# Three pairs of blocks taken through a two-level Strassen–Winograd feed-forward in lockstep, with every weight product streamed from DRAM

## The chip, the cores and the metric

The kernel runs on one core of a Trainium2 chip. The metric is the device time of that core in microseconds, as the median of three runs. Each version also has one profiled execution, whose span (first to last instruction) and own time stand beside the median below. In the profile PE is TensorE's matmuls, PEld its weight loads (which overlap the matmuls), DVE is VectorE, ACT ScalarE, POOL GpSimd and SP SyncE. All arithmetic is fp32. Names such as `x`, `h`, `t` and `r` are tiles in SBUF; `m`, `a`, `b` and `c` are PSUM pools.

## The reference

A linear attention without a softmax, then a gated feed-forward network, on 8 sequences of 576 positions with 8 heads of 64. The two are joined by laying the heads side by side.

```python
kv  = np.einsum('bhsd,bhse->bhde', k, v)          # one 64x64 matrix per sequence and head
out = np.einsum('bhsd,bhde->bhse', q, kv)
rms = np.sqrt(np.mean(out * out, axis=-1, keepdims=True) + 1e-06)
x   = (out / rms * g_norm).transpose(0, 2, 1, 3).reshape(4608, 512)
g   = x @ w_gate                                   # [4608,512] @ [512,1536]
val = x @ w_val
res = (g * (1.0 / (1.0 + np.exp(-g))) * val) @ w_out   # [4608,1536] @ [1536,512]
```

## The kernel before

**Blocks.** The 4608 tokens are worked in nine blocks of 512 (`NB = 9`, `BLK = 512`), numbered 0 to 8. For each block there is an `Att` object, which makes the block's `x` [512 features × 512 tokens, features on the partitions], and an `Ffn` object, which has an *up* part (gate and value products, silu, their product `h`) and a *down* part (`h @ w_out`). Blocks run one after the other; while block n's feed-forward runs, pieces of block n+1's attention are put between its products.

**Strassen–Winograd.** A product of 2 × 2 blocks of matrices can be made with seven smaller products instead of eight, at the price of sums of the operands and of the results. The kernel's up does this at no level for block 0 (`plain_up`, line 1026: matmuls with 512 columns of tokens, in two runs of 256), at one level for block 1 (class `Up`, line 587: 256 columns), and at two levels from block `DEEP = 2` on (class `Inner`, line 660). At two levels there are 49 products of 128 × 128 × 128, each named by an outer number and an inner number from 1 to 7. For one pair `d` of the six 128-wide weight columns, `Inner` runs four groups of outer products, `GROUPS = ((1, 5), (6, 2), (7,), (4, 3))`, and in each group the inner products 1, 5, 6, 2 and 7 with 3 and 4 of the group before put in between (`sequence`, line 701). The product with outer `o` and inner `p` has a leaf of the weights as its stationary operand (`weight`, line 704) and a leaf of x as its moving operand of 128 columns (`operand`, line 712). It is done for the two columns f = 0, 1 of the pair. So one step of a group with two outers makes four products, which fill one PSUM bank of 512 columns. Inner products accumulate in three chains of PSUM tiles, `a`, `b` and `c`. A finished bank is moved out by ScalarE for group 0 and by an add on VectorE for the others (`multiply`, line 719: the `L111` and `L742` rows of the profile), and the last combinations (`made1` to `made3`) run on GpSimd and ScalarE. The final one writes `h` and its sums `s1`.

**Down.** One level, seven products of 12 matmuls with 256 columns (line 565, of class `Quad`; class `Down`, line 855). Three of them (5, 7, 4) need differences of `w_out`, which `turn_t` makes on GpSimd, for each block anew, in tiles of the pool `t`. During down the next block's attention is finished: `fill[p]()` in `Ffn.down` (line 998) runs the steps that `Att.steps` names. After product 1 come the heads (line 361), the squares, the root of the norm, its scaling and a transpose on VectorE; after product 5, `place_x` issues 16 DMAs that put the 32 × 32 pieces of the transposed x in place, eight of them on SP and eight on ScalarE's queue; after product 2, `end` applies the gain and makes the sums of x that both Strassen levels need (`sums`, line 443), which end in the tiles `x` and `xi`.

**Weights.** The original leaves and the sums of the four outer numbers 1, 6, 2, 3 with inner 1, 6, 2, 3 are resident in `wg` and `wv`. The other 33 leaves of each column live in DRAM, written by block 1 (`leaf_steps`, line 829), and are streamed for every block. Class `Stream` (line 787) holds a queue of chunks of mostly 256 KB, 17 per pair of columns, in the order of use (`CHUNKS`). The pool `t` has nine tiles of this size. `pump` (line 801) issues one DMA on SP for each tile that has come free; it is called after every product. `enable` opens a block's chunks after product 7 of the down before.

**What sets the order.** Every engine takes its instructions in the order of the program, as the scheduler lays it out from the code and the explicit `issue_after` constraints. TensorE thus takes products, k/v visits (`visit`: `kv`, line 305, whose matmuls are at line 316) and heads in a fixed order. SP takes all loads in one order: weight chunks (line 809), k and v (`load_kv`, line 257), q and the stores of results (line 953). q comes by `load_quarters` (line 271, the DMA at line 284): 32 DMAs for a block, in pieces of 32 positions × 32 of a head's 64 elements. `load_q` issues all 16 of one half; in block 2's up block 4's q is issued in four lots of about eight. Afterwards block n+2's q is issued together ahead of block n's down. In block 1's up, block 3's q is issued after the second k/v visit.

**Room.** `x` and `xi` come from the pool `x`, `h` from the pool `h`, each with one buffer, so the next block's x is written when the last product of this block's up has been read, in down.

## Time and profile before

| | |
|---|---|
| runs | 1020.94, 1022.35, 1024.27 us; median 1022.35 us |
| profiled execution | 1020.91 us, its span 1019.1 us |
| granted TensorE clock | 0.999 |
| matmul instructions | 8522 |
| VectorE, GpSimd, ScalarE instructions | 1169, 280, 353 |
| moved by DMA | 170.26 MB, 167 GB/s in the mean |
| weight chunks (`t<-w`) of 256 KB | 336, 3.5 us from issue to landing |

Of the stretches of the trace, block 2's up runs from 269.5 us to 338.9 us and its down to 377.1; the next blocks begin their up at 377.1, 484.4, 591.8, 699.0, 808.8 and 913.3 us, so that a block takes 107.3 us in blocks 3, 4 and 5, 109.7 in block 6 and 104.5 in block 7. The last down ends at 1015.7 us.

How to read it: the busy table counts an instruction from start to end, and since matmuls are pipelined with modelled ends, the distance between the starts of two of them is the better price of one. A row of the timeline has the start in microseconds, the length of the run of like instructions, engine, line, operation, tile written and read, sizes and count; a time in brackets with an arrow is idle time before it and what released it. SPq are the DMAs that SP issues, and their length there is the time that SP needs to issue them, not the time until the data have landed. In the group rows, "L728 PE" is the two-level up, "L565 PE" the one-level up and all downs. Line 111 is the helper for sums, line 112 that for differences and line 113 that for products, so their rows gather many places; the tile names tell them apart.

### The profile page before, as it was taken

The page shows a single profiled execution, that of the slowest core. Times are in us where ns is not written, and L with a number is a line of the kernel's source. Part 1 is how long each engine was busy: PE and PEld are TensorE (multiplying, and loading weights), DVE is VectorE, ACT ScalarE, POOL GpSimd, SP SyncE. Part 2 cuts the span into 40 slices and gives each one's busy share as a digit, 9 for nine tenths or more (in the row PEclk, how much of TensorE's full clock was granted, in tenths as well). Part 3 has the DMA queues.
Part 4 walks back from the last instruction along what each step waited for, and adds up shares of the span by engine and source line. Part 5 has one row for each costly group of instructions (what it writes and reads, how often), then busy time and mean ns, then how long its engine had stood idle before and what let it go on. Part 6 is the DMA issues. An engine that isn't in the chain of part 4 may idle for free.

```text
span 1019.1 us, 21397 instructions
## 1 busy us (share of the span) xinstructions
PE 1003.5 (98%) x8522; PEld 895.9 (88%) x8522; DVE 700.9 (69%) x1169; ACT 228.1 (22%) x353; POOL 368.9 (36%) x280
## 2 busy tenths in 40 slices
PE   6999999999999999999999999999999999999998
PEld 4544688888999899998999899988998999989997
DVE  3999688998666946685558566665668466946661
ACT  2765112121211221221121111111121211221110
POOL 0000263534055503561246315630555045513670
PEclk9999999999999999999999999999999999999999
DMA  8689643767888277846685568646772766066601
GB/s 238 202 257 273 119 81 109 188 165 159 251 231 244 50 195 202 248 83 147 206 234 136 101 207 241 168 62 194 233 201 44 182 191 192 22 169 199 194 25 42
DMA packets 273844, 170.26 MB, mean 167 GB/s; under 512 B 150608, under 2 KB 241872, under 8 KB 273744
## 3 DMA queue, kind: packets, MB, share of 16 engines
q1 hardware_dynamic: 238800, 164.42, 59.1%
q10 hardware_dynamic: 34880, 4.46, 2.7%
q8 instruction: 68, 1.11, 0.5%
q14 instruction: 32, 0.26, 0.1%
q0 software_dynamic: 64, 0.00, 0.0%
HBM read 138.02 MB, written 22.41 MB: 157 GB/s over the span
## 4 chain that ended last, share of the span: by engine, by line
PE 90%; DVE 6%; DMA 2%; issue 1%; ACT 1%; SPq 0%; DVEq 0%; ACTq 0%
PE b L728 26%; PE b L565 19%; PE c L728 13%; PE c L565 10%; PE a L728 6%; PE a L565 5%; PE b L1035 4%; PE c L1035 4%; PE m L361 1%; PE m L316 1%; DVE r L112 1%; DVE r L111 1%; DVE xi L112 1%; DMA h<-in_v_dram 1%; DVE t L112 1%
## 5 line engine op out<-in xcount | busy, mean ns | idle before, releaser
L111 POOL TENSOR_TENSOR r<-r 128x256 f32<-128x256 f32 (+1 forms) x105 | 110.7, 1061 | 295.2 <-DVE r L111 292.9
L111 DVE TENSOR_TENSOR r<-b,r 128x512 f32<-128x512 f32 (+1 forms) x273 | 161.9, 605 | 64.9 <-PE b L728 60.4
L112 POOL TENSOR_TENSOR t<-wo 128x512 f32<-128x512 f32 x81 | 114.4, 1436 | 211.9 <-DVE wo L111 102.6
L111 DVE TENSOR_TENSOR r<-c,r 128x512 f32<-128x512 f32 (+1 forms) x179 | 108.3, 616 | 89.1 <-PE c L728 58.2
L728 PE MATMUL b<-x,t 128*128 128x128 f32 x1092 | 151.2, 275 | 0.0
L111 DVE TENSOR_TENSOR r<-a,r 128x512 f32<-128x512 f32 (+1 forms) x99 | 62.4, 630 | 113.1 <-PE a L565 71.2
L728 PEld LDWEIGHTS b<-x,t 128*128 128x128 f32 x1092 | 136.5, 192 | 0.8 <-DVE r L111 0.2
L728 PE MATMUL c<-xi,t 128*128 128x128 f32 x840 | 112.4, 275 | 1.0 <-DVE xi L111 1.0
L113 POOL TENSOR_TENSOR h<-r 128x1024 f32<-128x1024 f32 (+1 forms) x40 | 82.4, 2075 | 82.2 <-DVE r L111 79.2
L728 PEld LDWEIGHTS c<-xi,t 128*128 128x128 f32 x840 | 102.9, 192 | 1.2 <-DVE xi L111 1.2
L565 PE MATMUL b<-wo,h 128*128 128x256 f32 x432 | 100.1, 383 | 0.1
L565 PE MATMUL b<-t,h 128*128 128x256 f32 x432 | 96.2, 379 | 0.0
L565 PEld LDWEIGHTS b<-t,h 128*128 128x128 f32 x432 | 82.0, 190 | 11.3 <-issue 0.2
L565 PEld LDWEIGHTS b<-wo,h 128*128 128x128 f32 x432 | 79.8, 190 | 13.2 <-DVE h L113 2.5
L742 ACT COPY r<-b 128x512 f32<-128x512 f32 x63 | 36.9, 585 | 214.9 <-PE b L728 208.1
L728 PE MATMUL b<-xi,t 128*128 128x128 f32 x588 | 79.7, 276 | 0.0
L728 PEld LDWEIGHTS b<-xi,t 128*128 128x128 f32 x588 | 72.4, 192 | 0.0
L728 PE MATMUL b<-x,wg 128*128 128x128 f32 x336 | 52.8, 279 | 0.2 <-DVE x L112 0.2
L728 PE MATMUL b<-x,wv 128*128 128x128 f32 x336 | 51.2, 275 | 0.0
L565 PE MATMUL a<-wo,h 128*128 128x256 f32 x216 | 48.3, 379 | 0.0
L565 PE MATMUL c<-t,s 128*128 128x256 f32 x216 | 48.1, 379 | 0.0
L565 PE MATMUL c<-wo,h 128*128 128x256 f32 x216 | 48.1, 379 | 0.0
(133 smaller groups left out, 1562.2 us busy)
## 6 DMA issues: line engine op xcount, KB each, us to landing
t<-w SPq DMA_DIRECT2D x336, 256.0 KB, 3.5
out_dram<-r SPq DMA_DIRECT2D x17, 512.0 KB, 3.1
ld<-in_k_dram SPq DMA_DIRECT2D x26, 288.0 KB, 4.9
ld<-in_v_dram SPq DMA_DIRECT2D x26, 288.0 KB, 5.8
ld<-in_moe_w_gate_dram SPq DMA_DIRECT2D x12, 512.0 KB, 4.7
ld<-in_moe_w_val_dram SPq DMA_DIRECT2D x12, 512.0 KB, 4.6
ld<-in_moe_w_out_dram SPq DMA_DIRECT2D x12, 512.0 KB, 5.0
w<-t SPq DMA_DIRECT2D x18, 256.0 KB, 3.0
```

The source lines that it names most:

```text
L111: add = lambda e, o, a, b: e.tensor_tensor(out=o, in0=a, in1=b, op=OP.add)
L112: sub = lambda e, o, a, b: e.tensor_tensor(out=o, in0=a, in1=b, op=OP.subtract)
L113: mul = lambda e, o, a, b: e.tensor_tensor(out=o, in0=a, in1=b, op=OP.mult)
L316: self.positions = nc.tensor.matmul(self.kv_ps[r][u * D : (u + 1) * D, g, :], lhsT=k[:, u, c, :], rhs=v[:, u, c, :], start=(c == 0), stop= ...
L361: self.multiplied = nc.tensor.matmul(self.ps[i][u][p : p + D, t, j, :], lhsT=self.qt[rows, 2 * i + t, j, p : p + D], rhs=kvs[b % 3][rows, ...
L565: self.ffn.multiplied = nc.tensor.matmul(banks[e][:, e], lhsT=lhsT, rhs=rhs, start=first and i == 0 and (e == 0 or banks[0] is not banks[1 ...
L728: self.ffn.multiplied = nc.tensor.matmul(ps[:, i, f], lhsT=self.weight(o, p, f), rhs=self.operand(o, p), start=first and (i, f) == (0, 0), ...
L742: nc.scalar.copy(out=dst, in_=ps)
L1035: nc.tensor.matmul(t, lhsT=w[f // 2][:, i, P * (f % 2) : P * (f % 2 + 1)], rhs=x[:, i, of], start=(i == 0), stop=(i == NS - 1),)
```

## The change

Blocks 0, 1 and 2 are still taken alone. Blocks 3 and 4, 5 and 6, 7 and 8 are each taken by a new class `Pair`: their ups run in lockstep, then the first block's down, then the second's.

**Joint products.** `Joint`, a subclass of `Inner`, makes one matmul per outer and inner product, whose moving operand is 256 columns: 128 tokens of the first block and 128 of the second. It works on one weight column `j` at a time, where `Inner` did two. A step of a group with two outers still fills a bank of 512 columns. What `Inner` has as its two weight columns is in `Joint` the two blocks, so the moves out of PSUM keep their shapes.

**Arena.** x, `xi` and `h` of both blocks must lie at a fixed distance to be one operand. They are now parts of one tile `arena` of 97 KiB per partition. In blocks 0 to 2 it holds `wg` and `wv` (48 KiB), then one x, one xi and one h; from block 3 on two slots of x with xi and two of h take the place, also of the resident weights. Of block 3's attention, three temporary tiles are given homes in there (`place`, `homes`).

**All leaves streamed.** Block 1 writes all 49 leaves of each column to DRAM, in an order by outer and inner number. Block 2 reads them in the chunks `ALONE`, which are the old `CHUNKS`; since a chunk's pieces of the two columns now lie apart, most chunks need two DMAs of 128 KB instead of one of 256 KB. The pairs read chunks `JOINT`, 14 for each column.

**Attention.** Block 3's is done within block 2's up (`ahead`), at its fills 1 to 10 of 12: two k/v visits, the turning of q, its heads in two halves, and its x turned by TensorE (`turn_x`) instead of VectorE and DMA. Block 4's k/v visit is in block 2's up and the rest of its attention in block 2's down. In a pair's up, the k/v of the two blocks of the next pair is visited after units 6 and 13 of 24 and their q is issued in eight lots of about eight after units 14 to 21; then the first down finishes the attention of the next pair's first block, the second down that of its second. Block 3's q, which was issued in block 1's up, is issued after block 1's down has been laid out. The inner sums of block 3's x come in block 2's down after product 1.

**Down.** The first down of a pair keeps its three tiles of differences of `w_out` (`keeps`) and the second uses them again; the second opens the stream of the next pair. The sums of the second block's h are made on GpSimd after product 5 of the first down (`second_sums`).

```diff
-    x_pool = pool("x", 1)
-    h_pool = pool("h", 1)
...
-    wg, wv = ([consts.tile([P, NS, 2 * P], F32, name=f"{x}{j}") for j in range(NP)] for x in ("wg", "wv"))
+    arena = consts.tile([P, 97 * KIB], F32, name="arena")
...
+    both = span(0, 2 * SLOT).rearrange("p (b y) -> p b y", b=2)
+    x_both = both[:, :, 0 : X * KIB].rearrange("p b (o k t) -> p b o k t", o=7, k=2)
+    xi_both = both[:, :, X * KIB :].rearrange("p b (a l c) -> p b a l c", a=3, l=7)
+    h_both = span(2 * SLOT, 2 * H_).rearrange("p (b f t) -> p b f t", b=2, f=NF)
+    PAIRED = 3
...
+        def targets(self, ps, o, p):
+            return [(ps[:, f], self.weight(o, p, f)) for f in range(2)]
...
-                for f in range(2):
+                for to, weight in self.targets(ps[:, i], o, p):
                     self.ffn.multiplied = nc.tensor.matmul(
-                        ps[:, i, f], lhsT=self.weight(o, p, f), rhs=self.operand(o, p),
-                        start=first and (i, f) == (0, 0), stop=True, skip_group_check=True,
+                        to, lhsT=weight, rhs=self.operand(o, p), start=begins, stop=True, skip_group_check=True,
...
+    class Joint(Inner):
+        def targets(self, ps, o, p):
+            return [(ps, stream.use(self.ffn.n, self.d, o, p))]
+        def operand(self, o, p):
+            x = XO[o]
+            if p in XI:
+                return xi_both[:, :, XI[p], x]
+            i, q = {1: (0, 0), 2: (1, 0), 6: (0, 1), 4: (1, 1)}[p]
+            return x_both[:, :, x, i, P * q : P * (q + 1)]
...
+    JOINT = [((1, 5), ps) for ps in ((1, 6), (5,), (2, 3), (7, 4))]
+    JOINT += [((6, 2), ps) for ps in ((1, 6), (5,), (2, 3), (7, 4))]
+    JOINT += [((7,), (1, 6, 2, 3)), ((7,), (7, 4, 5))]
+    JOINT += [((4, 3), ps) for ps in ((1, 6), (5,), (2, 3), (7, 4))]
...
         def pump(self):
             while self.next and not self.held[-9]:
...
+                if n == DEEP:
...
+                    if k - i < 2:
+                        src = flat[:, 2 * d : 2 * d + 2, i : k + 1].rearrange("p f l c -> p f (l c)")
+                        nc.sync.dma_start(out=tile_[:, :, 0 : count * P], in_=src)
+                        continue
+                    for f in range(2):
+                        nc.sync.dma_start(out=self.tiles[key][:, f], in_=flat[:, 2 * d + f, i : k + 1 : k - i])
+                    continue
+                os, ps = JOINT[c]
...
+                nc.sync.dma_start(out=to, in_=src)
...
-            if os[0] not in RESIDENT:
-                yield lambda t=t, o=os[0]: send((o, 1), 4, t[:, 0].rearrange("p i e c -> p (i e) c"))
-            yield lambda b11=b11, t2_=t2_, to=to: sub(nc.vector, to[:, :, 1], b11, t2_)
-            yield lambda i=i, n=n, o=os[0]: send((o, 4), 3 * n, room[:, i : i + 3 * n])
+            yield lambda t=t, os=os: send(os, (1, 6, 2, 3), t.rearrange("p o i e c -> p o (i e c)"))
+            yield lambda b11=b11, t2_=t2_, to=to: sub(nc.vector, to[:, :, 0], b11, t2_)
+            yield lambda to=to, os=os: send(os, (7, 4, 5), to.rearrange("p o r c -> p o (r c)"))
...
+    class Pair:
...
+        def up(self, fill):
...
+            for j in range(NP):
+                shared = {}
+                units += [Joint(self, j, g, shared) for g in range(4)]
...
+            a.down_ = Down(a)
+            a.down_.keeps = True
+            a.down_.turn_t(5)
...
+        def second_sums(self):
...
+            for j in range(0, NP, 2):
+                b.ended = b.h_sums(j, 2, nc.gpsimd)
+            b.down_ = Down(b)
+            b.down_.t = self.a.down_.t
+            b.down_.opens = self.n + 2 if self.n + 2 < NB else None
...
+    def ahead(ffn, att):
...
+        def half(i):
+            with tc.issue_after(ffn.multiplied.ins):
+                att.half(i, (m_psum, m_psum))
+            ffn.visited = att.multiplied
...
+        return {
+            1: start, 3: turn, 4: finish, 5: lambda: half(0), 7: second, 8: last, 9: lambda: turn_x(0),
+            10: lambda: turn_x(1),
+        }
...
+        ffn.down(nxt, {1: blocks[PAIRED].inner_sums} if n == 2 else {})
+        if n == 1:
             for i in range(2):
-                blocks[n + 2].load_q(i)
-        ffn.down(nxt)
+                blocks[PAIRED].load_q(i)
...
+    for n in range(PAIRED, NB, 2):
+        pair = Pair(n)
...
+            fill = {6: first_kv, 13: second_kv}
+            for i in range(8):
+                fill[14 + i] = lambda i=i, after=after: after[i // 4].load_quarters(i % 4 // 2, (i % 2,))
+        pair.up(fill)
...
+        pair.a.down(after[0] if after else None, {5: pair.second_sums})
...
+        pair.b.down(after[1] if after else None)
```

## The prediction

> **What bounds the kernel now.** I read the page's busy table first, then TensorE's timeline, then SP's queue.
>
> ```profile
> span 1019.1 us, 21397 instructions
> PE 1003.5 (98%) x8522; PEld 895.9 (88%) x8522; DVE 700.9 (69%) x1169; ACT 228.1 (22%) x353; POOL 368.9 (36%) x280
> PE 90%; DVE 6%; DMA 2%; issue 1%; ACT 1%; SPq 0%; DVEq 0%; ACTq 0%
> ```
>
> TensorE is busy 98% of the span, and the chain that ended last is 90% TensorE. After 34 us its timeline shows only four gaps with a cause, the longest 1.04 us. So a time follows from what TensorE must stream, plus new gaps. The means of the group table (275 ns at 128 columns, 379 at 256) have modelled ends and would promise far too much; the price is the distance of starts:
>
> ```profile
> 484.42 0.61 PE L728 MATMUL b<-x,wg 128*128 128x128 f32 x4
> 484.86 0.61 PE L728 MATMUL b<-x,t 128*128 128x128 f32 x4
> 485.31 1.06 PE L728 MATMUL c<-xi,t 128*128 128x128 f32 x8
> 486.20 0.66 PE L728 MATMUL b<-x,wg 128*128 128x128 f32 x4
> ...
> 565.85 5.34 PE L565 MATMUL c<-t,s 128*128 128x256 f32 x24
> 571.03 1.24 PE L565 MATMUL b<-t,h 128*128 128x256 f32 x5
> ```
>
> One fp32 product is two such instructions. Eight of 128 columns take 486.20 - 485.31 = 0.89 us, 0.2235 us a product; 24 of 256 columns take 5.18 us, 0.4317 us a product. Two narrow products cost 0.447 us, one wide one 0.432: a gain of 15.3 ns, 3.4%, no more.
>
> SP's queue, where every weight block, q and k/v load is issued in order:
>
> ```profile
> 265.60 2.94 SPq L809 DMA_DIRECT2D t<-w  x3
> 271.81 0.39 SPq L953 DMA_DIRECT2D out_dram<-r  x1
> 272.30 2.33 SPq L809 DMA_DIRECT2D t<-w  x3
> 274.68 0.43 SPq L284 DMA_DIRECT2D ld<-in_q_dram  x1
> ...
> 334.18 17.69 SPq L284 DMA_DIRECT2D ld<-in_q_dram  x32
> ...
> 656.13 26.25 SPq L284 DMA_DIRECT2D ld<-in_q_dram  x32
> 682.49 5.80 SPq L434 DMA_DIRECT2D x<-r  x8
> ```
>
> Block 2's up starts at 269.49. SP stores block 1's last result at 271.81 and at once fetches the next weights. A block's 32 q loads occupy SP for 17.69 us (0.553 each); before block 6, 26.25 us (0.82), because some waited. That made block 6's x late, and TensorE paid for it:
>
> ```profile
> 704.03 2.05 PE L728 MATMUL c<-xi,t 128*128 128x128 f32 x16 [1.04 <-DVE xi L111]
> ```
>
> Block 6's first stretch of up, from 699.03 to its k/v visit at 721.61, takes 22.6 us where block 3's takes 20.3: 2.3 us.
>
> **What the Trainium skill says.** "TensorE: Matmul & The Clock Gate", sections "LDWEIGHTS (loading the stationary operand)" and "Wait — 56ns, not 53.3ns?": loading 128 columns takes 128/1.2 = 107 ns, streaming N takes N/2.4 + 2.5. The trace agrees: 111.8 ns per narrow instruction, near the load, and 215.8 per wide one, which is the streaming price for 512. So the narrow form is already near the load's limit and only a little is left. "HAM oscillation — how this bites in real kernels" there: idle beyond 3.4 us puts the array at half clock. The trace's start shows it: 64x64 products 36 ns apart at 10 to 12 us, 17.8 ns later. "DMA: Bandwidth & Descriptors", "Anatomy of one DMA": a wait is served on the issuing sequencer, and a fixed 2 us or so is mostly completion (told there of GpSimd's path). SP's weight loads agree: 2.3 us to landing at least, 3.5 median.
>
> **The change part by part.** Sums are against the profiled execution: span 1019.1, its own time 1020.91; the median of the runs is 1022.35, to which I add the difference in span.
>
> *Wide products.* Three pairs, 6 weight columns, 49 products: 882 wide ones for 1764 narrow: 882 x 15.3 ns = -13.5 us. The moving operand becomes two runs of 128, one per block. The plain up of block 0 already moves two runs of 256: 3.43 us per 8 instructions of 512, 429 ns, full rate.
>
> *Block 6's late x.* q for a pair is now loaded inside the pair's up, no longer just ahead of the x copies: -2.3 us.
>
> *Block 3 on TensorE.* Its x is turned by 16 transposes, not by VectorE and DMA. Eight took 1.07 us at line 410: +2.1 us. Its heads and k/v products, and block 4's k/v, only move.
>
> *Evictions in pairs.* As many, of the same shapes. Backlogged, VectorE starts one of 512 every 0.61 us and one of 256 every 0.335; per weight column 17 and 7, 12.7 us under 21.2 us of TensorE (49 x 0.432). The tightest step is 0.335 under 0.432: hidden, at 0.1 us a step if it weren't.
>
> *Stream in pairs.* 49 leaves of 64 KB per column are 152 GB/s; before, 16.5 chunks of 256 KB in 21.9 us, 197 GB/s. It is hidden better. q pieces: 8 x 0.553 + 3.5 chunks x 0.4 = 5.8 us of SP per unit of 5.3 us, over 8 units 4 us behind; the nine tiles hold 13.6 us of work, less 3.5 for landing. Hidden; 4 us a pair if that cover is spent.
>
> *Leaf stores in block 1.* All 49 leaves go out, 6.3 MB more, where the page's slices show 81 to 188 GB/s against 273 at best. Hidden by slack of the queues; 0 to 3 us if leaf room comes free late. I take 0.
>
> *Second block's sums.* Six GpSimd operations of about 1.3 us, after a.down's product 5, with 20 us to its end: hidden.
>
> *Block 3's q, the step I think decides.* It was loaded in block 1's up. Now it follows block 1's down. In the order in which the changed program issues, two of its 32 DMAs go early; 30 stand after block 1's last store and ahead of block 2's tenth chunk. The store waits for the end of down, as at 271.81. So SP is free at 272.3, the 30 cost 30 x 0.553 = 16.6 us, to 288.9; a chunk is now mostly two DMAs, 0.9 us; landing 2.3 to 3.5: 292.1 to 293.3. TensorE stands there after 60 narrow products and one k/v visit: 13.4 + 1.3 = 14.7 us, at 284.2. Nothing hides the rest, as products wait in order: 7.9 to 9.1 us, I take 8.5. It goes on at half clock for about 3.6 us, losing 1.8. Then four k/v loads (0.63 each) stand before chunk 11, which lands near 296.5, and TensorE asks for it at 296: +0.7. Together +11 us. What comes next has room: 42 chunks of 1.6 DMAs at 0.4 us, 12 k/v loads, block 4's 32 q loads and the burst are 27 + 7.6 + 17.7 + 16.6 = 69 us of SP in an up of some 76. Bounds: at the median 0.449 per q load 5 us of stall, at 0.82 about 17.
>
> *Attention of block 3 inside block 2's up.* VectorE gets 2 transposes (2.5 us), 4 reduces (2.5), 2 roots (3.5 each), 4 scales (2.4), 8 sums (7): 22 us beside 38 of evictions, in 76. It fits on average, mostly one operation at a time between evictions. But VectorE is in order and an eviction has about 0.9 us before TensorE's product 6 needs it; a reduce waits for heads and squares. 0 to 5, I take +2.
>
> Sum: -13.5 - 2.3 + 2.1 + 11 + 2 = -0.7. Span 1018.4, median 1021.6.
>
> **Rivals.** (B) *The burst is covered.* SP's quickest q load took 0.31 us; below 0.29 a load chunk 9 is in time. Or the queue reaches the burst early. For it: a stall of 8 us never occurred before. Against: 32 in 17.69 with the DMA engines only 36% busy, so issue is the limit. Then -13.5 - 2.3 + 2.1 + 2 = -11.7, 1010.6.
>
> (C) *SP is block 2's bound: slower.* One mechanism: a q load costs 0.82, as before block 6, with the engines also moving twice as many half-size weight packets and 2.4 MB more k/v. The burst lasts 24.6, chunk 9 lands near 300.7, a stall of 16.5; block 4's q then leaves no room to catch up, some 3 more. -0.7 + 8 + 3 = +10.3, 1032.6. It decides from 0.68 us a load. For it: 15 q loads took 11.08 us (0.74) beside weight stores; 69 of 76 us are already booked. Against: the first loads of the burst meet little other traffic.
>
> (D) *The gain isn't there.* Two runs in operands a column of memory apart could cost more. Block 0 speaks against it; then 1035. I count it in C.
>
> **How the numbers follow.** My forecast (A), stall and gain about cancelling, 0.46, own range 1016 to 1028; B 0.23; C with D 0.31. Within 0.3% (3.1 us, about what a measurement here can tell) lies 0.27 of A; 0.11 of A is faster and 0.08 slower. So faster 0.34, same 0.27, slower 0.39. The range cuts a tenth at either end of B and C: 1009 to 1034.
>
> **What would show it.** Right: wide products 0.432 us apart, a pair's up near 127 us plus its visits; 30 q loads after block 1's last store, TensorE waiting some 8 us on a weight tile 15 us into block 2's up; no gap before block 6. Wrong: no such gap, then B; several gaps of over 2 us on weight tiles through block 2, then C; regular gaps of tenths in the pairs (evictions), or waits on block 1's stores, would be mechanisms that I priced at nothing.

## The result: 1.7% slower, and the profile after

The changed kernel takes 1039.38 us (median of 4 runs, 1038.53 to 1040.75) where the kernel before, beside it, takes 1022.11: a ratio of 1.0168, with a 95% interval from 1.0147 to 1.0188. The forecast was 1021.6, with a range up to 1034. The profiled execution took 1040.75 us, so it is the slowest of the four, 1.4 us above the median; its span is 1039.0 us. That of before is 19.9 less, and since its execution was 1.2 us below the median, the two spans are further apart than the medians (17.3).

From the page of the changed kernel, the span and the busy table:

```profile
span 1039.0 us, 17769 instructions
PE 998.8 (96%) x6774; PEld 843.6 (81%) x6774; DVE 685.2 (66%) x1166; ACT 228.6 (22%) x355; POOL 359.6 (35%) x283
```

There are 1748 TensorE instructions fewer (two each for 882 products, less 16 transposes), and TensorE stands idle 40 us, where it stood 16. The place is found by cutting both spans at the same points of the work: block 2, blocks 3 and 4, 5 and 6, 7 and 8. Columns: stretch, its length, busy time and instructions of TensorE, its weight loads, VectorE, ScalarE and GpSimd, then the granted clock, the share of the DMA engines and their rate. Before:

```profile
269.50:377.10 107.60, 107.58 (x1030) 102.00 (x1029) 70.92 (x113) 20.40 (x30) 42.80 (x32) 1.00 0.70 182
377.10:591.80 214.70, 214.65 (x2058) 203.84 (x2057) 139.99 (x223) 40.80 (x60) 85.62 (x64) 1.00 0.65 174
591.80:808.80 217.00, 215.73 (x2058) 204.13 (x2057) 142.16 (x226) 40.70 (x60) 86.18 (x64) 1.00 0.63 167
808.80:1015.70 206.90, 206.88 (x1641) 196.92 (x1639) 123.59 (x195) 35.68 (x50) 85.47 (x64) 1.00 0.46 132
```

After:

```profile
269.90:415.30 145.40, 122.39 (x1318) 114.45 (x1317) 92.35 (x154) 25.33 (x40) 44.58 (x32) 0.92 0.73 176
415.30:628.80 213.50, 211.44 (x1470) 182.83 (x1469) 137.21 (x221) 40.57 (x60) 82.39 (x65) 1.00 0.57 143
628.80:835.50 206.70, 206.70 (x1325) 181.37 (x1324) 136.11 (x220) 40.36 (x58) 82.29 (x65) 1.00 0.49 125
835.50:1035.60 200.10, 200.10 (x925) 175.15 (x923) 100.22 (x160) 31.42 (x44) 82.07 (x65) 1.00 0.33 99
```

The three pairs are 1.2, 10.3 and 6.8 us shorter, 18.3 in all. Block 2 is 37.8 us longer, with its clock at 0.92. So the gain came, and block 2 lost twice as much.

**The pairs.** The wide products start as foreseen. From the timeline of TensorE in pair 7+8 (start, length, engine, line, operation, tiles, sizes, count):

```profile
840.85 1.89 PE L761 MATMUL c<-arena,t 128*128 128x256 f32 x8
842.58 1.89 PE L761 MATMUL b<-arena,t 128*128 128x256 f32 x8
```

Eight instructions in 1.73 us, 0.4325 us a product. Of the 18.3 us, 13.5 are the wide products, 2.3 the late x before block 6, which is gone, and 4.4 is work that now lies in block 2 (the k/v visit and the heads of one more block, 2.3 and 2.1); three small gaps in pair 3+4 (0.92 on a weight tile, 0.75 and 0.39) take 2.1 back. That makes 18.1.

**Block 2.** TensorE's gaps there, each with its releaser:

```profile
285.37 0.71 PE L761 MATMUL b<-arena,t 128*128 128x128 f32 x4 [0.86 <-DVE r L132]
296.52 2.20 PE L761 MATMUL b<-arena,t 128*128 128x128 f32 x8 [10.44 <-DMA t<-w]
...
305.33 1.19 PE L761 MATMUL b<-arena,t 128*128 128x128 f32 x4 [4.89 <-DMA t<-w]
...
332.69 2.81 PE L761 MATMUL b<-arena,t 128*128 128x128 f32 x12 [3.39 <-DVE r L132]
...
362.92 1.38 PE L761 MATMUL b<-arena,t 128*128 128x128 f32 x10 [0.64 <-DVE r L132]
...
369.82 0.71 PE L761 MATMUL b<-arena,t 128*128 128x128 f32 x4 [0.89 <-DVE r L132]
...
381.35 1.99 PE L593 MATMUL b<-wo,arena 128*128 128x256 f32 x8 [1.09 <-DVE arena L134]
```

With one more of 0.79 at 365.98 that is 15.3 us on weight tiles and 7.7 us on VectorE. After each of the three longest TensorE runs slower; windows as above, right behind each of them:

```profile
296.50:300.40 3.90, 3.88 (x16) 3.56 (x16) 1.41 (x3) 0.84 (x1) 0.72 (x1) 0.50 0.99 257
305.30:309.40 4.10, 4.07 (x20) 4.10 (x21) 0.90 (x2) 0.00 (x0) 0.00 (x0) 0.53 1.10 291
332.70:339.00 6.30, 6.30 (x164) 6.14 (x164) 2.56 (x6) 1.06 (x1) 1.46 (x2) 0.73 0.48 133
```

These granted clocks cost 3.9 x 0.50 + 4.1 x 0.47 + 6.3 x 0.27 = 5.6 us: 3.9 behind the weight tiles, 1.7 behind VectorE. Together with the work that moved here (4.4) and the 16 transposes (0.88 + 0.87) this is 34.8 of the 37.8 us; 3 us I don't assign.

**SP's queue** at the start of block 2 (q loads and k/v loads are what stands between the weight chunks at lines 894 and 897):

```profile
275.98 0.43 SPq L1049 DMA_DIRECT2D out_dram<-r  x1
276.47 17.26 SPq L312 DMA_DIRECT2D ld<-in_q_dram  x30
293.82 0.92 SPq L897 DMA_DIRECT2D t<-w  x2
294.84 0.41 SPq L894 DMA_DIRECT2D t<-w  x1
295.35 1.34 SPq L294 DMA_DIRECT2D ld<-in_k_dram  x2
296.74 1.25 SPq L294 DMA_DIRECT2D ld<-in_v_dram  x2
298.03 0.59 SPq L894 DMA_DIRECT2D t<-w  x1
```

The 30 q loads stand where the prediction put them, at 0.575 us each, but begin at 276.47 and not at 272.3. From 256.0 on SP issues one DMA behind another, with pauses of about 0.1 us (the lengths hold waits on a tile or a landing too): 24 from there to the burst, eight leaf stores, fourteen weight loads and two result stores. Before there were 14 up to the last result store at 271.81, with pauses of 1.6 and 3.3 us. And what the DMA engines do meanwhile, 270 to 330 us in 40 slices of 1.5 us, busy tenths and rate:

```profile
DMA  9999898314343434589999999999999999999998
GB/s 396 390 372 261 222 374 176 63 27 70 62 71 62 73 60 71 105 248 230 247 237 217 256 316 287 300 251 223 244 217 250 290 239 207 229 231 252 308 284 270
```

During the burst the engines are a third busy at some 65 GB/s: SP's issue is the limit. Behind it they are full for 30 us, and what is asked for lands later. The commonest weight chunk of these 60 us, with the size and the median time from issue to landing, after and then before:

```profile
t<-w SPq DMA_DIRECT2D x30, 128.0 KB, 5.7
t<-w SPq DMA_DIRECT2D x39, 256.0 KB, 3.6
```

Full engines alone make no stall: in the same 60 us the kernel before moved 14.3 MB, the changed one 13.0, and before, TensorE waited on no weight tile. What differs is the lead that the nine weight tiles give: the burst has used it up, and chunk 11 is issued from 298.03 us on, 2.4 us before TensorE asks for it (300.4). No step of mine had this second half.

### The profile page after: what moved, and what is told of

Read it like the earlier page. It is cut to its first block, busy times and chain, and to the rows that moved or that the text cites. A ratio compares the mean times of both kernels' runs of the same rounds, so it can differ in the third digit from the quotient of the medians.

```text
span 1039.0 us, 17769 instructions
## 1 busy us (share of the span) xinstructions
PE 998.8 (96%) x6774; PEld 843.6 (81%) x6774; DVE 685.2 (66%) x1166; ACT 228.6 (22%) x355; POOL 359.6 (35%) x283
## 4 chain that ended last, share of the span: by engine, by line
PE 70%; DMA 3%; SPq 2%; DVE 1%; issue 0%; ACT 0%; DVEq 0%; ACTq 0%
PE b L761 23%; PE b L593 16%; PE c L761 11%; PE c L593 8%; PE a L761 6%; PE a L593 4%; DMA t<-w 2%; PE m L389 1%; PE m L344 1%; SPq L312 1%; DVE r L132 1%; DMA out_dram<-r 1%; SPq L897 0%; DVE arena L134 0%; SPq L294 0%
## 5 line engine op out<-in xcount | busy, mean ns | idle before, releaser
L761 PE MATMUL b<-arena,t 128*128 128x256 f32 (+1 forms) x1248 | 281.8, 365 | 21.9 <-DMA t<-w 15.3
L761 PEld LDWEIGHTS b<-arena,t 128*128 128x128 f32 x1248 | 223.1, 193 | 53.0 <-DMA t<-w 10.6
L761 PE MATMUL c<-arena,t 128*128 128x256 f32 (+1 forms) x624 | 140.0, 362 | 0.7 <-ACT r L775 0.7
L132 DVE TENSOR_TENSOR r<-a,r 128x512 f32<-128x512 f32 (+1 forms) x99 | 62.5, 631 | 107.9 <-PE a L593 66.6
L134 POOL TENSOR_TENSOR arena<-r 128x1024 f32<-128x1024 f32 (+1 forms) x46 | 96.1, 2103 | 87.7 <-DVE r L132 75.9
L761 PEld LDWEIGHTS c<-arena,t 128*128 128x128 f32 x624 | 111.9, 193 | 14.3 <-ACT r L775 1.2
L133 DVE TENSOR_TENSOR arena<-arena 128x512 f32<-128x512 f32 (+3 forms) x101 | 102.4, 1026 | 18.2 <-PE b L593 12.1
L593 PE MATMUL b<-wo,arena 128*128 128x256 f32 x432 | 98.8, 382 | 2.3 <-DVE arena L134 1.5
L593 PE MATMUL b<-t,arena 128*128 128x256 f32 x432 | 96.3, 380 | 0.0
L593 PEld LDWEIGHTS b<-wo,arena 128*128 128x128 f32 x432 | 81.1, 190 | 13.9 <-DVE arena L134 1.8
L593 PEld LDWEIGHTS b<-t,arena 128*128 128x128 f32 x432 | 82.0, 190 | 11.4 <-POOL s L132 0.2
## 6 DMA issues: line engine op xcount, KB each, us to landing
t<-w SPq DMA_DIRECT2D x198, 256.0 KB, 3.2
```

What stands on the lines that cost most here:

```text
L132: add = lambda e, o, a, b: e.tensor_tensor(out=o, in0=a, in1=b, op=OP.add)
L133: sub = lambda e, o, a, b: e.tensor_tensor(out=o, in0=a, in1=b, op=OP.subtract)
L134: mul = lambda e, o, a, b: e.tensor_tensor(out=o, in0=a, in1=b, op=OP.mult)
L593: self.ffn.multiplied = nc.tensor.matmul(banks[e][:, e], lhsT=lhsT, rhs=rhs, start=first and i == 0 and (e == 0 or banks[0] is not banks[1 ...
L761: self.ffn.multiplied = nc.tensor.matmul(to, lhsT=weight, rhs=self.operand(o, p), start=begins, stop=True, skip_group_check=True,)
```

## The experiments

Each run is beside runs of the kernel before on the same chip (medians 1021.6 to 1022.1); "changed" is the changed kernel, 1039.4.

| kernel | median us | ratio to before, 95% |
|---|---|---|
| changed, products narrow again | 1051.63 | 1.0288 (1.0270 to 1.0306) |
| changed, 16 of block 3's q ahead of block 1's down | 1037.42 | 1.0146 (1.0128 to 1.0165) |
| changed, k/v of block 2's up on ScalarE's queue | 1049.13 | 1.0274 (1.0242 to 1.0306) |
| changed, block 3's second k/v one unit later | 1036.46 | 1.0146 (1.0132 to 1.0160) |
| changed, 20 weight issues for 27 | 1033.83 | 1.0121 (1.0106 to 1.0136) |
| no burst (16 q on SP, 16 on ScalarE, early) | 1029.26 | 1.0070 (1.0051 to 1.0088) |
| no burst, root spread, all sums on GpSimd | 1033.01 | 1.0110 (1.0091 to 1.0129) |
| no burst, root ordered one by one | 1030.93 | 1.0089 (1.0073 to 1.0105) |
| no burst, k/v on ScalarE's queue | 1037.09 | 1.0153 (1.0137 to 1.0168) |
| the same, root ordered one by one | 1038.01 | 1.0162 (1.0144 to 1.0180) |
| the same, outer sums on GpSimd | 1038.96 | 1.0169 (1.0153 to 1.0186) |
| no burst, 20 issues | 1023.43 | 1.0017 (1.0010 to 1.0024) |
| no burst, 20 issues, root one by one, sums in down | 1029.88 | 1.0078 (1.0059 to 1.0097) |
| no burst, 20 issues, sums late | 1020.48 | 0.9986 (0.9979 to 0.9992) |
| the same, k/v of block 4 later | 1021.71 | 0.9997 (0.9988 to 1.0005) |
| no burst, 20 issues, sums late, block 3's k/v later | 1019.17 | 0.9979 (0.9970 to 0.9989) |

### Are the wide products worth what was said?

```diff
-                    self.ffn.multiplied = nc.tensor.matmul(
-                        to, lhsT=weight, rhs=self.operand(o, p), start=begins, stop=True, skip_group_check=True,
...
+                    for to_, rhs in self.parts_of(to, self.operand(o, p)):
+                        self.ffn.multiplied = nc.tensor.matmul(
+                            to_, lhsT=weight, rhs=rhs, start=begins, stop=True, skip_group_check=True,
...
+        def parts_of(self, to, x):                                # class Joint: two of 128, same weight tile
+            return [(to[:, b], x[:, b]) for b in range(2)]
```

> The changed kernel, but each joint product of 256 columns is made as two of 128 with the same weight tile, one per block; 1764 narrow products in place of 882 wide ones, nothing else. If a wide product saves 15.3 ns against two narrow ones, as read from the trace of before: 882 x 15.3 ns = 13.5 us more than the changed kernel, about 1053. Rival (two runs of memory in an operand make the wide product dearer, so that the saving is less than half): at most 6 us more, 1046 or less.

Measured 1051.63, 12.3 us above the changed kernel. That is 13.9 ns a product for 15.3. An operand in two runs of memory costs nothing that shows: rival (D) is out, and the step holds.

### Is it the burst?

The half of block 3's q loads ahead of block 1's down, and then all of them with the second half on ScalarE's queue:

```diff
             nxt.turn()
             blocks[PAIRED].load_kv(0)
+            blocks[PAIRED].load_q(0)
+            blocks[PAIRED].load_quarters(1, queue=nc.scalar)      # second kernel only
...
         if n == 1:                                                # these three lines go in the second kernel
-            for i in range(2):
-                blocks[PAIRED].load_q(i)
+            blocks[PAIRED].load_q(1)                              # first kernel only
```

> The changed kernel with the first 16 of block 3's 32 q loads issued ahead of block 1's down; 16 stay behind it. Theory (SP's issue of the burst sets block 2's first stall of 10.4 us): 14 fewer loads of 0.575 us in the burst, so the stall is 2 to 3 us and TensorE keeps its full clock after it, some 2 us more: about 1029. If the second stall (4.9 us) comes from the four k/v loads that stand ahead of the next chunks it stays; if it is what is left of the burst's backlog it goes too: about 1023. Rival (the stall is the bandwidth of the DMA engines, or late leaf stores, not the queue's order): both stalls stay, 1038 to 1040.

Measured 1037.42, only 2 us less, as neither theory said. The timeline of TensorE in it:

```profile
274.52 1.16 PE L761 MATMUL c<-arena,t 128*128 128x128 f32 x8 [2.47 <-DVE arena L132]
276.74 1.19 PE L761 MATMUL b<-arena 128*128 128x128 f32 x4 [1.06 <-DVE arena L133]
...
301.12 1.19 PE L761 MATMUL b<-arena,t 128*128 128x128 f32 x4 [5.25 <-DMA t<-w]
```

The first stall is gone, as expected of the burst. But the 16 loads now took 17.1 us of SP. SP's waits in them, from 236 to 253 us (in total, times, longest):

```profile
SPq L312 <- DMA arena<-r: 6.1, 1, 6.1
```

Most of what they took above 0.575 each is one wait of 6.1 us on a piece of block 2's x that ScalarE's queue places. In the program's instructions, the DMAs of both queues take turns on the same eight completion semaphores, and a q load waits until the eighth DMA before it has landed; one of the q loads had that piece as its eighth, and the piece itself was issued only at 248.46. SP's own pieces of x, behind the q loads, thus started at 255.0 instead of 248.8, the sums of x came late, and block 2 began with 4.3 us of gaps on `arena` and half clock behind them. The stall moved ahead of the block.

> The changed kernel with all of block 3's q loads ahead of block 1's down, 16 on SP and 16 on ScalarE's queue, so that no q load stands between block 2's first weight chunks. Theory: the first stall is 0 and its half clock gone. With a second stall of 4.9 us that belongs to the k/v loads about 1026; if that was backlog of the burst, about 1020. What VectorE costs (8 us of gaps in block 2) stays in either case. Rival (bandwidth or late leaf stores): no change, 1038 to 1040.

Measured 1029.26, 10.1 us less than the changed kernel. The gap of 10.44 us is 0; x is in time (0.77 us more in block 1's down). What is left on weight tiles:

```profile
287.73 0.68 PE L761 MATMUL a<-arena,t 128*128 128x128 f32 x4 [1.00 <-DMA t<-w]
293.23 0.68 PE L761 MATMUL b<-arena,t 128*128 128x128 f32 x4 [3.93 <-DMA t<-w]
```

So the burst was 10 us, and most of the second stall (3.93 us of 4.89) was not its backlog. The time is 3 us above the 1026 expected for this case.

### What is the second stall?

The k/v loads of block 2's up on another queue, burst left in place:

```diff
-                    nc.sync.dma_start(                 # load_kv
+                    queue.dma_start(                   # nc.scalar for the twelve of block 2's up
```

> The changed kernel, the burst of 30 q loads left as it is; only the twelve k and v loads in block 2's up (the second of block 3, both of block 4) are issued by ScalarE's queue in place of SP's. Theory (the second stall, 4.9 us at the chunk behind the first four k/v loads, is SP's time for them and the wait for their completion): the first stall of 10.4 us stays, the second falls to 0 to 2 us: 1034 to 1037. Rival (the second stall is the burst's backlog): it stays, 1038 to 1041.

Measured 1049.13, worse by 9.8 us. The trace:

```profile
301.97 2.28 PE L761 MATMUL b<-arena,t 128*128 128x128 f32 x8 [14.99 <-DMA t<-w]
...
326.95 1.22 PE L761 MATMUL b<-arena 128*128 128x128 f32 x4 [6.13 <-ACT r L775]
```

A load that waits on ScalarE's queue holds up the evictions behind it (6.13 us), and the burst itself took 21.9 us of SP, not 17.3: SP waited 5.4 us on landings in it, and 1.2 in the changed kernel. In the program, q loads of the burst now stand behind k/v loads of the other queue on the shared semaphores. The trace gives other q loads as what SP waited for in 4.8 of the 5.4 us, so that the k/v loads lengthened the burst is likely and not shown. The run doesn't answer its question. Without the burst it was the same:

> No burst (all of block 3's q ahead of block 1's down, half of it on ScalarE's queue) and the twelve k/v loads on ScalarE's queue too. Theory: both stalls on weight tiles in block 2 gone (3.9 and 1.0 us with the burst alone removed, and about 1.5 us of half clock): 1022 to 1024. Rival (SP has too little time for the weight chunks in block 2's first 25 us whatever stands between them): a stall of 2 us or more on a weight tile stays, 1026 to 1029.

Measured 1037.09, 7.8 us more than without this edit: a stall of 4.93 us on a weight tile and one of 5.38 us on ScalarE's eviction, and more than either expectation. The cleaner edit keeps SP and only moves the four loads behind five chunks:

```diff
         def start():
             visit(ffn, att, (0,))
-            att.load_kv(1)
...
+        def late_kv():                                # at fill 2, start is at fill 1
+            with tc.issue_after(ffn.multiplied.ins):
+                att.load_kv(1)
```

> The changed kernel, burst left as it is; the four loads of block 3's second k and v are issued one unit later, behind five more weight chunks, on SP as before. Theory (they are what makes the next chunk late after the burst): the first stall of 10.4 us stays, the second of 4.9 us falls to 0 to 2 us, and block 3's second k/v visit may wait up to 2 us: 1034 to 1037. Rival (the DMA engines are busy without a pause after the burst, whatever the order): as many microseconds are lost in later waits, 1038 to 1041.

Measured 1036.46, 2.9 us less. The first stall stays (9.84 us), the second is gone (0.36), and 2.39 us come back on a weight tile at 317.75. Both theories hold in part: the order put 4.9 us at that point, and of these about half only moved, as the rival expected of engines without a pause. VectorE's gap of 3.39 us is 0.92 in this run, though its work was not touched; more on that below. With it the gaps of block 2 add up to 5.2 us less, and I don't assign the 2.3 us of them that don't show in the time.

### How many issues?

Block 2's chunks in fewer DMAs: the leaves in the order 1, 6, 2, 3, 4, 7, 5, and two neighbours of one outer number in a chunk.

```diff
-    OUTERS, INNERS = (1, 5, 6, 2, 7, 4, 3), (1, 6, 2, 3, 7, 4, 5)
+    OUTERS, INNERS = (1, 5, 6, 2, 7, 4, 3), (1, 6, 2, 3, 4, 7, 5)
-        ((5, 1), (5, 6)), ((1, 5), (5, 5)), ((5, 2), (5, 3)), ((1, 7), (5, 7)), ((2, 5), (6, 5)), ((1, 4), (5, 4)),
+        ((5, 1), (5, 6)), ((1, 7), (1, 5)), ((5, 7), (5, 5)), ((5, 2), (5, 3)), ((6, 7), (6, 5)), ((2, 7), (2, 5)),
+        ((1, 4), (5, 4)),
...
```

> The changed kernel, burst and all, with the leaves in DRAM ordered 1, 6, 2, 3, 4, 7, 5 and block 2's chunks paired so that 14 of 17 are one DMA of 256 KB and 3 are two of 128 KB: 20 issues in place of 27 for each pair of columns. Theory (SP issues without a pause from block 1's last stores on, so every issue ahead of the burst delays it by 0.4 to 0.5 us): some 5 issues fewer ahead of the burst and 2 between burst and second stall, both stalls together 3 to 4 us shorter: 1035 to 1036. Rival (the number of issues does not matter, bytes and landing do): no change.

Measured 1033.83, 5.6 us less: the two stalls are 6.92 and 2.32 us. More than expected; the edit also doubles the runs of memory that those chunks are read in (1 KB for 512 bytes), so the number of issues and the form of the transfers aren't told apart.

> The kernel without burst (16 of block 3's q loads on SP, 16 on ScalarE's queue, all ahead of block 1's down; k/v on SP as in the changed kernel) with the 20 issues for 27. Theory: its remaining stall of 3.9 us is SP's time at block 2's start, so it falls to 0 to 2 us and the half clock behind it goes: 1024 to 1026. Rival (the stall is the wait for the completion of the k/v loads): it stays at 3 to 4 us, 1028 to 1030.

Measured 1023.43, 5.8 us less than without the burst alone. The two causes add up: 10.1 + 5.6 = 15.7 of the measured 16.0.

### VectorE

The gap of 3.39 us in the changed kernel, seen from the two engines. Lines 412 to 421 are the root, 132 and 133 sums:

```profile
323.88 1.27 POOL L132 TENSOR_TENSOR s<-arena 128x512 f32<-128x512 f32 x1
324.43 0.75 DVE L412 TENSOR_SCALAR y<-z 128x16 int32<-128x16 int32 x1
328.36 0.16 DVE L421 SCALAR_TENSOR_TENSOR y<-a,y 128x16 f32<-128x16 f32 x1
328.52 0.73 POOL L132 TENSOR_TENSOR r<-r 128x256 f32<-128x256 f32 x1 [2.02 <-DVE y L421]
328.56 0.72 DVE L419 SCALAR_TENSOR_TENSOR a<-y 128x16 f32<-128x16 f32 x1
```

An operation of the root takes 0.16 to 0.18 us, but where a sum of GpSimd runs beside it, it ended when that sum ended: 0.75 and 0.72 us here, and 0.83 and 0.72 in two more, 2.3 us of the 3.39. Evictions, which read PSUM, took 0.69 us at most with or without GpSimd. The next runs took the gap for operations packed between evictions.

> As the kernel with 16 loads on ScalarE's queue, and in addition VectorE's work for block 3's attention is thinned out: the root and the scaling come one operation per product, and the sums of block 3's x run on GpSimd. Theory (VectorE's gaps in block 2, 7.7 us and the half clock after the longest, are attention in front of evictions): 6 to 9 us less than that kernel. Rival (they are what is left of the stalls, evictions bunched up behind a late start): already gone in that kernel, and no difference here.

Measured 1033.01, 3.8 us more. The gap, 2.78 us without this edit, was 3.40: the scheduler had put the root's operations back where they were. And the sums of x on GpSimd came in front of its part of the last h, and block 4's heads waited 7.31 us in down. Next, each operation was tied behind an eviction:

```diff
+            for step in att.root_steps(i) + att.scale_steps(i):
+                ffn.making.extend([lambda step=step: late(step)] + 3 * [lambda: None])   # late: issue_after(ffn.evicted.ins)
```

> The kernel without burst, k/v on SP, two-DMA chunks, with the root and the scaling of block 3 ordered one by one behind further evictions. Theory: its gap of 2.8 us on VectorE falls below 1 us and its half clock goes: 3 to 5 us less than without the spreading, 1025. Rival (VectorE short of time altogether, or the scaling late for k/v of block 4): the gaps move and add up to the same, 1028 to 1031.

Measured 1030.93, 1.7 us more than without, which is within the intervals of the two: no gain is what it shows. The gap of 2.8 us fell to 0.64, and 1.84 and 2.23 us appeared later, as the rival said. In this trace eight operations of the root, spread to where GpSimd is at work, took 0.32 to 1.79 us (four were lengthened in the changed kernel), up to the end of its operation. This edit and the other ones that spread the root also put both turns of x one fill later, nearer to the end of up, so that what spreading alone does isn't shown. Two more runs put it on the kernel whose k/v are on ScalarE's queue, and tell little, since that kernel is held up by its queue:

> As the kernel without burst and with k/v on ScalarE's queue, and each operation of block 3's root and scaling is ordered behind one more eviction of its own, so that VectorE never has several of them in a row. Theory (the gap of 2.8 to 3.4 us is the root and scaling packed between evictions): that gap is below 1 us and the half clock behind it gone, 3 to 5 us less than without the spreading. Rival (VectorE is short of time altogether there): the gap splits into several that add up to the same, no gain.

> As the kernel with spread root, and the outer sums of block 3's x (four operations of 512 columns) on GpSimd; the inner sums stay on VectorE. Theory: the three gaps of 0.6 to 0.9 us near the end of block 2's up are these sums in front of evictions, about 2 us less than with VectorE's sums. Rival (GpSimd's sums are later and slow its other work, as they did with the inner sums moved too): 1 to 5 us more.

Measured 1038.01 and 1038.96, for 1037.09 without either: no difference clear of the noise.

> No burst, 20 issues for 27, root and scaling spread, and the sums of block 3's x moved from the end of block 2's up into its down behind product 5. Each of the three is to save what it does alone (4, 4 and 2 us): 1018 to 1021, faster than the kernel before or even with it. Rival (each fix uncovers the next wait): 1024 or more.

Measured 1029.88, 6.5 us more than without the two, as the rival said. The scheduler brought the sums forward, in front of h, and block 4's heads waited 3.93 us; what belongs to the root and what to the sums isn't told apart. With the sums held back for certain, and the root as it was:

```diff
-            if i == 1:
-                att.sums()
...
+        def sums_late(nxt=nxt):                                   # at product 5 of block 2's down
+            with tc.issue_after(nxt.blocked.ins):                 # block 4's last transpose
+                blocks[PAIRED].sums()
+                blocks[PAIRED].inner_sums()
```

> No burst and 20 issues for 27, and the outer and inner sums of block 3's x are ordered behind the transposes of block 4's attention in block 2's down, where VectorE waits for block 4's x to be placed. Theory (the sums stand in front of the evictions and of h at the end of block 2's up and slow GpSimd's differences of the output weights): the gap of 0.6 us near the end of up, the 1.8 us before the first down product and the two of 0.5 us go, 3 to 3.5 us less than without: 1020. Rival (they come in front of block 4's own sums and make pair 3+4 late): 1023 to 1028.

Measured 1020.48, 3.0 us less, as expected. So the sums of block 3's x cost 3 us where they stood, 0.57 of it a wait on GpSimd's differences of `w_out`.

> The same with block 4's eight k/v loads issued together after the fifth unit of block 2's up, in place of after the third and the fourth. Theory (each lot of four k/v loads takes 2.7 us of SP ahead of the next chunk): the gap of 1.4 us on a weight tile goes too, 1018 to 1019, some 0.3% below the kernel before. Rival (k/v then land too late for their visit after the seventh unit): a new gap there of 1 to 4 us, 1020 to 1024.

Measured 1021.71, 1.2 us more than without, and no gain: a gap of 2.12 us on a weight tile stayed where it was, since it is block 3's k/v that stands ahead of it. Those were moved in the last run:

> No burst, 20 issues for 27, block 3's sums late, and block 3's second k/v loads one unit later. Theory: the gap of 2.1 us on a weight tile at block 2's start, and 1.2 us of half clock behind it, go: 1017 to 1018. Rival (the engines' backlog only moves): 1020 to 1022.

Measured 1019.17, between the two expectations, and 0.9979 of the kernel before (0.9970 to 0.9989): 0.2% less than it, clear of the noise, but not clear of the kernel without this last edit (0.9979 to 0.9992). Its gaps in block 2, all of 0.5 us or more:

```profile
293.61 1.26 PE L344 MATMUL m<-ld 64*64 64x64 f32 x36 [0.80 <-DMA ld<-in_v_dram]
303.64 0.71 PE L761 MATMUL c<-arena,t 128*128 128x128 f32 x4 [1.63 <-DMA t<-w]
313.75 0.71 PE L761 MATMUL b<-arena,t 128*128 128x128 f32 x4 [0.67 <-DMA t<-w]
360.15 1.99 PE L593 MATMUL b<-wo,arena 128*128 128x256 f32 x8 [1.08 <-DVE arena L134]
```

No gap on an eviction is left in its up, with the root unspread. Moving the k/v visit moves the heads and the root against the work of the other engines: here one operation of the root took 0.72 us and one 0.35, all others 0.18 or less. In the changed kernel such operations lost 2.3 us to GpSimd's sums, here 0.8. By the traces VectorE's longest gap was thus for the most part GpSimd's doing; no run moved GpSimd's sums alone, which would prove it. The DMA engines are still full from 270 to 315 us in it, and of the 18 us that the pairs gain about 2.4 reach the end.

## Why the prediction was wrong

By its own steps:

- **Wide products, −13.5**: right, 12.3 by the run that undoes it. **Block 6's late x, −2.3**: right. **Transposes, +2.1**: 1.75. **Second block's sums, leaf stores' effect in block 1**: right; block 2 begins at 269.90 where it began at 269.49. **Stream and evictions in pairs**, priced at 0: 2.1 us, all in pair 3+4.
- **Block 3's q, the mechanism**: right in place, kind and price of a load. Taking the burst away gave 10.1 us. **Its size, +11, is the term that failed**: 15.3 us of stall and 3.9 of half clock behind it, 19.2 us. Three parts of it were short. (1) "SP is free at 272.3" took the time of before's last store for SP's time; the leaf stores and the doubled weight issues that I had costed as hidden stand in that queue, and the burst began at 276.47. TensorE was 1.9 us later too, so the stall was 10.4 and not 8.5. (2) "Chunk 11 lands near 296.5: +0.7" counted only SP's time. TensorE had it at 305.3, behind 1.2 MB of k and v (four loads of 288 KB) in engines that were full: 4.9. (3) Half clock, 1.8 us, was counted once; behind the two stalls it cost 3.9.
- **"What comes next has room: 69 us of SP in an up of some 76"**: no weight tile was late after chunk 11, so the queue had room. But room on the queue's clock says nothing of the time to landing behind the burst, and the DMA engines, on which I made no sum, were full for 30 us.
- **Attention of block 3 on VectorE, +2, the second term that failed**: 7.7 us of gaps and 1.7 of half clock, 9.4. I had priced each operation as if VectorE were alone, with an average of "22 us beside 38 of evictions, in 76". Of the gaps, 2.3 us are operations of the root that lasted until a sum of GpSimd beside them had ended. The sums of x, counted in the same average, came at the end of up, in front of the evictions and of h; holding them back gave 3.0 us. The other gaps stay open.

The sum: −13.5 became −12.3, +11 became 19.2, +2 became 9.4, 0 became 2.1. With −2.3 and +1.8 that is +17.9, against 19.9 between the two spans.

Two readings of the trace in it don't hold as they stand. At the start of the trace the 64 x 64 products are 27 ns apart, not 36: 64 of them start from 10.10 to 11.83 us. And that the narrow form is limited by the load is not shown: half of the wide 215.8 ns is 107.9 ns, as near to 111.8 as the load's 107. The gain of 15.3 ns, which is measured, doesn't rest on either.

Of the rivals, (B) failed on the burst: it isn't covered. (C) had the direction, and of its signs the "several gaps of over 2 us on weight tiles through block 2" (two of them); but its mechanism was a dearer q load, which decides from 0.68 us on, and the load cost 0.575. So the slower side came true below the point that I had named for it. The 0.82 us was no price of a load either: of the 26.25 us, 9.5 are one wait on a piece of block 6's x from ScalarE's queue (as with the 16 loads above) and 4.2 one on VectorE. That wait is also what made block 6's x late in the kernel before, since SP's own pieces of it stood behind.

What stands above on where q was issued before is wrong in part. Block 3's q was not asked for in block 1's up, nor block 4's in four lots. The kernel before asks for block 3's q in four lots in block 2's up; in the order as laid out, 16 stood at the start of block 1's down (the row with 15 loads in 11.08 us that I cite under (C)) and 16 came one to six at a time between block 2's chunks, as at 274.68. In block 1's up it asks for block 2's q, and for block 4's together, ahead of block 2's down. The kernel before was thus the spread form of the burst, without a stall on a weight tile in block 2.

## What to carry to other kernels

When a change moves loads, write out the queue around the place with all its issues, those too that were costed as hidden, and let the burst begin where that queue lets it; then ask what lead is left behind it, and price the landings there as the full engines give them (5.7 us here), not as the median of the whole run (3.5). A gain spread over three pairs (18 us) was lost at one seam that had to prepare them (38 us), so a restructuring is priced at its seams first. Work moved to another queue or engine to relieve the first is worth a look at what waits there: of the four edits that did so with k/v or with sums, none gained, while half of block 3's q on ScalarE's queue, early, did.

## What the runs showed that I had not expected

- Half clock came after shorter gaps than the 3.4 us that the prediction had taken, and the length of one gap doesn't decide it. In the kernel without burst, with 20 issues and late sums, a gap of 2.13 us (one of 0.39 shortly before) was followed by 3.2 us at a clock of 0.55. In its predecessor, a gap of 1.74 us was followed by full clock, and one of 1.81 us (0.57 and 0.52 in the 6 us before) by 3.4 us at 0.55.
- SP's and ScalarE's queues are tied together by the program's eight completion semaphores. A q load on SP waited 6.1 us for a piece of x on ScalarE's queue in the kernel with 16 loads ahead, and 9.5 us in the kernel before, ahead of block 6.
- An operation of VectorE with its operands in SBUF can be held until an operation of GpSimd beside it has ended. In the 18 traces of this case the operations of the root, of 16 or 32 columns, never took more than 0.20 us with GpSimd idle (1826 of them); beside a GpSimd operation 98 of 143 took more than 0.3, up to 1.79 us, and each of these ended within 0.08 us of the end of GpSimd's. In the changed kernel evictions of 512 columns, which read PSUM, took 0.69 us at most with GpSimd at work or without. In the kernel with all sums on GpSimd, VectorE's sums of 128 x 512 at the start of block 2's down took 1.64 us while GpSimd had its own, where the same ones take 0.69 beside an idle GpSimd; and GpSimd's sums of 128 x 896 took 3.0 us there, 2.1 a little earlier, beside evictions.
- A q load of 24 or 40 KB cost SP 0.575 us in the burst. A longer mean of a row of such loads (0.82 before block 6, 1.07 in the kernel with 16 ahead) was one wait inside the row.
